# Moving setup evacuations, one filter copy and two output copies between VectorE, ScalarE and GpSimd in a fused FFT-filter and SwiGLU kernel

## The chip, the cores and the metric

The kernel runs on one core of a Trainium2 chip. The metric is the device time of one execution in microseconds (us); several executions are taken and their median is quoted. A trace comes from one profiled execution, and its "span" runs from the first to the last instruction, so that the time is some 1.7 to 2.4 us longer than the span.

In the profile the engines are called PE (TensorE matmuls), PEld (TensorE weight loads), DVE (VectorE), ACT (ScalarE), POOL (GpSimd) and SP (SyncE). A label such as L462 is a line of the kernel that was traced. The change adds three lines, so L569 of the kernel before is L572 of the changed one, and L578 is L581.

## The reference

Eight sequences of 3008 tokens with 256 features are filtered in the frequency domain. Each token then passes an RMS norm and a SwiGLU layer with 1536 hidden units.

```python
X = np.fft.rfft(x, axis=1)                      # x: 8 x 3008 x 256
y = np.fft.irfft(X * (filt_r + 1j * filt_i), n=3008, axis=1)
y = y.reshape(24064, 256)
xn = y / np.sqrt(np.mean(y * y, axis=-1, keepdims=True) + 1e-06) * rms_g
g = xn @ w_gate                                  # 256 x 1536
silu = g * (1.0 / (1.0 + np.exp(-g)))
out = (silu * (xn @ w_val)) @ w_out              # 1536 x 256
```

## The kernel before

The transforms are done in stages with small DFT matrices. For batch 0 they stand alone at the start ("the setup", up to some 60 us); those of the later batches are woven in between the SwiGLU matmuls of the batch ahead. The SwiGLU part takes the rest of the time and keeps TensorE full (in the trace below it is busy for 269.74 us of the 270 from 230 to 500 us).

In the setup, transposed groups `t1` are evacuated from PSUM to SBUF, stage B multiplies them on TensorE into `psb`, VectorE or GpSimd multiplies `psb` with the filter (`products`), and `bit_unit` (called by `inverses`) multiplies back on TensorE into `pgt`, which ScalarE evacuates into `gT`. The kernel keeps the filter on both halves of the partitions, so each chunk of it is duplicated by `f_dup`.

```python
def b_mm(b, i):                       # stage B of unit i
    ps = bank(3 if b else (0, 3, 4, 5)[i % 4], "psb").rearrange("p (a d) -> p a d", a=2)
    if b == 0 and i > 3:              # an idle matmul, overwritten by the real ones
        nc.tensor.matmul(ps[:, 0, :], wz[:, 0:P], wz[:, 0:D], start=True, stop=True)
    ...
def b_unit(b, i, ps=None):            # products of unit i
    ...
    eng = nc.vector
    if (i in (3, 5, 8, 12, 15)) if b else (i in (3, 7, 9, 12)):
        eng = nc.gpsimd
        ...
        nc.scalar.activation(out=v, in_=ps, func=AXT.Copy)   # GpSimd works on this copy
        ps = v
    eng.tensor_tensor(out=s1, in0=ps, in1=f1, op=ALU.mult)
    eng.tensor_tensor(out=s2, in0=ps, in1=f2, op=ALU.mult)
...
def f_dup(c, e, eng, lo=0, hi=KC):    # half of filter chunk c to the other partitions
    ...
    if eng is nc.scalar:
        eng.activation(out=t[a:a + HALF], in_=t[o:o + HALF], func=AXT.Copy)
    elif eng is nc.sync:
        eng.dma_start(t[a:a + HALF], t[o:o + HALF])
    else:
        eng.tensor_copy(out=t[a:a + HALF], in_=t[o:o + HALF])
...
def t1_copy(g, on_act):
    dst, ps = st[0]["t2"][g], st[0]["t2ps"].pop(g)
    if on_act:
        nc.scalar.activation(out=dst, in_=ps[0:KR], func=AXT.Copy)
    else:
        nc.vector.tensor_copy(out=dst, in_=ps[0:KR])
...
def down(b, m, jt, part):             # last matmul of a SwiGLU block
    ...
    if jt == JT - 1:
        o3 = late_p["op"].tile([P, 4, D], FP32, tag="o3", name="o3")
        if part is None:
            nc.scalar.activation(out=o3[:, 0:2, :], in_=po[0], func=AXT.Copy)
            nc.vector.tensor_copy(out=o3[:, 2:n, :], in_=po[1][:, 0:n - 2, :])
```

Of the kernel before, what the change touches and what calls it, by code (L numbers as in the profile page):

```python
# [12 lines left out]
AXT = mybir.ActivationFunctionType  # L13
# [108 lines left out]
def kernel(  # L122
# [11 lines left out]
    nc = tc.nc  # L134
# [109 lines left out]
    def b_unit(b, i, ps=None):  # L244
        if ps is None:
            ps = b_mm(b, i)
        f1, f2 = filt(2 * i, 2)
        if b:
            s1 = late_p["sp"].tile([P, 2, D], FP16, tag="s1", name="s1")
            s2 = late_p["sp"].tile([P, 2, D], FP16, tag="s2", name="s2")  # L250
            if summed(b, i):
                nc.vector.tensor_tensor(out=s1, in0=ps, in1=f1, op=ALU.mult)  # L252
                st[b]["s"][i] = (s1, s2, ps, f2)
                return
        elif i % 2:
            s1 = hp.tile([P, 512], FP16, tag="sg", name="sg").rearrange("p (a d) -> p a d", a=2)
            s2 = hhs[(i // 2) % 4].rearrange("p (a d) -> p a d", a=2)
        else:
            ss = xnp.tile([P, 2, 512], FP16, tag="xn", name="ss")
            s1, s2 = (ss[:, e, :].rearrange("p (a d) -> p a d", a=2) for e in range(2))  # L260
# [3 lines that stand above are left out]
            v = yp.tile([P, 2, 512], FP32, tag="y", name="v")  # L264
            v = v[:, 0, :].rearrange("p (a d) -> p a d", a=2)
            nc.scalar.activation(out=v, in_=ps, func=AXT.Copy)
# [3 lines that stand above are left out]
        st[b]["s"][i] = (s1, s2)  # L270
# [158 lines left out]
    def cut(b, m, part):  # L429
        return (0, nq(b, m)) if part is None else (2 * part, 2)  # L430
# [20 lines left out]
    def down(b, m, jt, part):  # L451
        hh = hh_of.pop((b, m, jt, part))
        if jt == 0:
            where = {None: ((psO, "po0"), (psO, "po1")), 0: ((psO, "po0"),), 1: ((psO, "po1"), (psM, "mx"))}
            po_of[(b, m, part)] = [pool.tile([P, 2, D], FP32, tag=tag, name=tag)
                                   for pool, tag in where[part]]
        po = po_of[(b, m, part)]

        n = cut(b, m, part)[1]
        per = 1 if part else 2  # L460
        for s4 in range(n):
            nc.tensor.matmul(po[s4 // per][:, s4 % per, :], hh[:, ts(s4, P)], wo[:, jt, :],  # L462
                             start=(jt == 0 and s4 % per == 0),
                             stop=(jt == JT - 1 and (s4 % per == per - 1 or s4 == n - 1)))
        if jt == JT - 1:
            o3 = late_p["op"].tile([P, 4, D], FP32, tag="o3", name="o3")
            if part is None:
                nc.scalar.activation(out=o3[:, 0:2, :], in_=po[0], func=AXT.Copy)
                nc.vector.tensor_copy(out=o3[:, 2:n, :], in_=po[1][:, 0:n - 2, :])  # L469
            else:  # L470
                nc.scalar.activation(out=o3[:, 0, :], in_=po[0][:, 0, :], func=AXT.Copy)
                nc.vector.tensor_copy(out=o3[:, 1, :], in_=po[part][:, 1 - part, :])
            po_of[(b, m, part)] = o3
# [38 lines left out]
    def f_dup(c, e, eng, lo=0, hi=KC):  # L512
        t = (fr, fi)[e][c][:, lo:hi, :]
        a, o = (0, HALF) if e else (HALF, 0)
# [6 lines that stand above are left out]
# [13 lines left out]
    def t1_mm(g):  # L534
        if g < 6:
            if g % 2 == 0:
                st[0]["t2t"] = t2p.tile([KR, KC, D], FP16, tag="t2", name="t2")
            dst = st[0]["t2t"][:, 4 * (g % 2):4 * (g % 2) + 4, :]
        else:
            dst = t3p.tile([KR, 4, D], FP16, tag="t3", name="t2")  # L540
        st[0]["t2"][g] = dst
        pool, tag = ((psG, "pg"), (psV, "pv"))[g % 2]
        ps = pool.tile([P, 4, D], FP16, tag=tag, name="pt1")
        af = aT.rearrange("p a k -> p (a k)")
        for a in range(4):
            for dh in range(2):
                b0 = dh * H * P
                src = af[:, b0:b0 + 32 * P].rearrange("p (i k) -> p k i", k=K2)[:, 4 * g + a, :]
                nc.tensor.transpose(ps[:, a, ts(dh, P)], src, ident)
        st[0]["t2ps"][g] = ps  # L550
# [8 lines that stand above are left out]
    def bit_unit(i):  # L559
        s1, s2 = st[0]["s"].pop(i)  # L560
        pair = i // 2
        closing = pair in st[0]["g"]
        if not closing:
            st[0]["g"][pair] = [bank((3 * dh) if pair == 7 else (1 + dh), "pgt") for dh in range(2)]
        for u in range(2):
            k = 2 * i + u
            for dh in range(2):
                o = st[0]["g"][pair][dh][:, ts(2 * (i % 2) + u, KR)]
                nc.tensor.matmul(o, s1[:, u, ds(dh * P, P)], wi_at(0, k)[:, 0:KR], start=True, stop=False)  # L569
                nc.tensor.matmul(o, s2[:, u, ds(dh * P, P)], wi_at(1, k)[:, 0:KR], start=False, stop=True)  # L570
        if closing:
            for dh in range(2):  # L572
                dst = gT[:, dh, pair * 4 * KR:(pair + 1) * 4 * KR]
                src = st[0]["g"][pair][dh][:, 0:4 * KR]
                if pair > 5 and dh:
                    nc.vector.tensor_copy(out=dst, in_=src)
                else:
                    nc.scalar.activation(out=dst, in_=src, func=AXT.Copy)  # L578
# [47 lines left out]
    def w_load(q):  # L626
        cols = ts(q, DFF // 3)
        for src, dst in ((moe_w_gate, wg), (moe_w_val, wv)):
            nc.gpsimd.dma_start(dst[:, :, cols], src.rearrange("(dt p) j -> p dt j", p=P)[:, :, cols])
        nc.gpsimd.dma_start(wo[:, ts(q, JT // 3), :],  # L630
                            moe_w_out.rearrange("(jt p) d -> p jt d", p=P)[:, ts(q, JT // 3), :])

    with tc.manual_schedule():
# [48 lines left out]
        A, G, S = nc.scalar, nc.gpsimd, nc.sync  # L682
        st[0]["t2ps"], st[0]["g"], psb = {}, {}, {}

        def products(*units):
            for i in units:
                b_unit(0, i, psb.pop(i))

        def stage_b(*units):
            for i in units:  # L690
                psb[i] = b_mm(0, i)

        def inverses(*units):
            for i in units:
                bit_unit(i)

        for g in range(4):
            t1_mm(g)
            t1_copy(g, g % 2)
        stage_b(0, 1, 2, 3)  # L700
        for g in range(4, 8):
            t1_mm(g)
        t1_copy(4, 0)
        f_dup(0, 0, A, 0, 2)
        f_dup(0, 1, G, 0, 2)
        f_dup(0, 0, A, 2, 4)
        f_dup(0, 1, G, 2, 8)
        f_dup(0, 0, A, 4, 8)
        products(0)
        stage_b(4)  # L710
        products(1)
# [23 lines left out]
        inverses(4)  # L735
        products(8)
        stage_b(12)
        inverses(5)
        f_dup(3, 1, A, 0, 4)
        products(12)  # L740
        w_load(0)
        w_load(1)
        products(10)
        stage_b(13, 14)
        inverses(6)
# [136 lines left out]
        for i in range(len(items) + 4):  # L882
            for fn, a in pre.get(i, ()):
                fn(*a)
            if i < len(items):
                gv(*items[i])
            for fn, a in plan.get(i, ()):
                fn(*a)
            if 2 <= i < len(items) + 2:
                down(*items[i - 2])  # L890
                if items[i - 2][2] == JT - 1:
                    stores[i + 1] = items[i - 2][:2] + items[i - 2][3:]
            for fn, a in late.get(i, ()):
                fn(*a)
            if i in stores:
                o_store(*stores[i])
# [30 lines left out]
```

## Time and profile before

| | kernel before |
|---|---|
| time, median of 3 executions | 889.63 us (889.43 to 890.09) |
| traced execution | 888.58 us, span 886.7 us |
| TensorE busy | 98% of the span |
| TensorE busy from 23.0 to 36.5 us | 8.83 of 13.5 us |
| TensorE waits for an output copy, whole span | 0.7 us, two times |

The page also divides the span into 40 slices. Of the kernel before I show the row of TensorE and the row of the granted clock, each digit a tenth of busy time or of full speed in one slice of some 22 us.

```profile
PE   8799999999999999999999999999999999999998
...
PEclk9999999999999999999999999999999999999999
```

Only the first two slices of TensorE and the last one are below 9: nearly all that can be won lies in the setup, with a few tenths in single places later.

### The profile page before, as it was taken

How to read it: one execution, taken by the hardware profiler on the slowest of the kernel's cores; microseconds unless marked ns; L12 is line 12 of the kernel's file. 1: busy time of each engine (PE TensorE's matmuls, PEld its weight loads, DVE VectorE, ACT ScalarE, POOL GpSimd, SP SyncE). 2: the span in 40 equal slices, each digit the busy share in tenths (PEclk: the TensorE clock that was granted, in tenths of full speed). 3: DMA queues.
4: the chain of work that ended last, by engine and by line, in shares of the span. 5: the costliest groups of instructions: out<-in, count | busy, mean ns of one | idle time of the engine just before them, and what ended most of it. 6: DMA issues, size and time to landing. Idle time of an engine off the chain costs nothing.

```text
span 886.7 us, 17463 instructions
## 1 busy us (share of the span) xinstructions
PE 873.2 (98%) x6257; PEld 559.0 (63%) x6257; DVE 678.7 (77%) x1088; ACT 625.3 (71%) x1069; POOL 436.5 (49%) x393
## 2 busy tenths in 40 slices
PE   8799999999999999999999999999999999999998
PEld 5566666666666666666666666666666666666556
DVE  7866786899888877888688887888878887555555
ACT  8878667677677766877677765887667765676444
POOL 7843941646527752667336661376515762155300
PEclk9999999999999999999999999999999999999999
DMA  9595736665653466343736346322352232222202
GB/s 201 118 197 156 163 78 209 143 141 122 177 141 82 101 141 173 93 100 101 193 86 143 85 90 183 93 91 84 99 152 75 64 90 71 77 66 49 72 24 48
DMA packets 80095, 101.44 MB, mean 114 GB/s; under 512 B 8108, under 2 KB 56684, under 8 KB 79560
## 3 DMA queue, kind: packets, MB, share of 16 engines
q1 hardware_dynamic: 69688, 84.23, 34.2%
q0 software_dynamic: 10240, 15.96, 11.5%
q8 instruction: 49, 0.80, 0.4%
q14 instruction: 38, 0.31, 0.1%
q10 hardware_dynamic: 80, 0.13, 0.1%
HBM read 67.67 MB, written 46.78 MB: 129 GB/s over the span
## 4 chain that ended last, share of the span: by engine, by line
PE 93%; DVE 1%; ACT 1%; issue 1%
PE po L462 27%; PE pg L443 27%; PE pv L443 27%; PE psi L291 3%; PE psb L238 3%; PE psn L323 2%; PE psa L203 2%; DVE o L469 1%; PE psq L352 1%; PE pt L589 0%; DVE hh L448 0%; ACT gT L578 0%; ACT fi L516 0%; PE psr L404 0%; PE pw L619 0%
## 5 line engine op out<-in xcount | busy, mean ns | idle before, releaser
L448 DVE TENSOR_TENSOR hh<-pv,sg 128x512 f16<-128x512 f32 (+2 forms) x588 | 392.8, 669 | 189.2 <-ACT sg L447 77.0
L447 ACT ACTIVATE sg<-pg 128x512 f16<-128x512 f32 (+2 forms) x588 | 340.8, 580 | 223.1 <-PE pg L443 213.6
L462 PE MATMUL po<-wo,hh 128*128 128x256 f16 x2244 | 342.6, 273 | 1.2 <-DVE o L469 0.7
L443 PE MATMUL pv<-xn,wv 128*128 128x512 f16 (+2 forms) x1176 | 339.9, 371 | 0.0
L443 PE MATMUL pg<-xn,wg 128*128 128x512 f16 (+2 forms) x1176 | 339.7, 370 | 0.0
L462 PEld LDWEIGHTS <-hh 128*128 128x128 f16 x2256 | 216.2, 97 | 96.8 <-issue 2.6
L282 POOL TENSOR_TENSOR s<-s,s 128x512 f16<-128x512 f16 x101 | 116.6, 1156 | 225.4 <-DVE s L276 156.6
L443 PEld LDWEIGHTS <-wv 128*128 128x128 f16 x1176 | 114.7, 98 | 128.9 <-issue 0.3
L419 POOL TENSOR_TENSOR xn<-y,rb 128x1024 f16<-128x1024 f32 (+1 forms) x45 | 126.1, 2802 | 52.5 <-DMA rb<-r_tmp 44.5
L443 PEld LDWEIGHTS <-wg 128*128 128x128 f16 x1176 | 111.2, 97 | 13.5 <-issue 0.3
L358 POOL TENSOR_TENSOR rho<-u,mhalf 128x4 f32<-128x4 f32 (+1 forms) x48 | 49.0, 1021 | 63.1 <-DVE u L356 62.9
L296 ACT ACTIVATE t<-psi 96x512 f16<-96x512 f32 x112 | 66.3, 592 | 8.3 <-PE psi L291 3.0
L276 DVE TENSOR_TENSOR s<-psb,fi 64x512 f16<-64x512 f32 x101 | 69.0, 683 | 3.0
L278 DVE SCALAR_TENSOR_TENSOR s<-psb,fi 64x512 f16<-64x512 f32 x101 | 69.9, 692 | 1.4
L329 ACT ACTIVATE y<-psn,gsb 128x512 f32<-128x512 f32 (+1 forms) x94 | 63.8, 678 | 7.8 <-PE psn L323 0.5
L252 DVE TENSOR_TENSOR s<-psb,fr 128x512 f16<-128x512 f32 x101 | 68.8, 681 | 0.0
L343 POOL TENSOR_TENSOR sq<-sq 128x512 f16<-128x512 f16 (+1 forms) x35 | 39.6, 1130 | 36.1 <-ACT sq L335 35.2
L335 ACT ACTIVATE sq<-psn 128x512 f16<-128x512 f32 (+1 forms) x94 | 54.8, 583 | 0.0
L208 ACT ACTIVATE t<-psa 128x512 f16<-128x512 f32 x70 | 41.8, 597 | 5.5 <-PE psa L203 2.4
L291 PE MATMUL psi<-s,wi 128*128 128x256 f16 x238 | 44.3, 273 | 0.0
L238 PE MATMUL psb<-t,wb 96*128 96x256 f16 x224 | 43.0, 273 | 0.3 <-DVE s L269 0.2
L323 PEld LDWEIGHTS <-t 128*128 128x128 f16 x368 | 28.3, 98 | 20.6 <-issue 0.4
(104 smaller groups left out, 526.2 us busy)
## 6 DMA issues: line engine op xcount, KB each, us to landing
out_dram<-o SPq DMA_DIRECT2D x83, 256.0 KB
xc<-in_x_dram POOLq DMA_DIRECT2D x56, 192.0 KB, 5.7
z_tmp<-t SPq DMA_DIRECT2D x28, 384.0 KB
t<-z_tmp SPq DMA_DIRECT2D x28, 384.0 KB
g_tmp<-t SPq DMA_DIRECT2D x56, 192.0 KB
rb<-r_tmp SPq DMA_DIRECT2D x41, 256.0 KB
t<-g_tmp SPq DMA_DIRECT2D x21, 384.0 KB
t<-g_tmp SPq DMA_DIRECT2D x7, 320.0 KB
```

Source lines behind the costliest of these rows:

```text
L238: nc.tensor.matmul(ps[:, u, :], w[:, k, :], t, start=True, stop=True)
L252: nc.vector.tensor_tensor(out=s1, in0=ps, in1=f1, op=ALU.mult)
L276: nc.vector.tensor_tensor(out=s2[a], in0=ps[e], in1=f2[e], op=ALU.mult)
L278: nc.vector.scalar_tensor_tensor(out=s2[a], in0=ps[e], scalar=-1.0, in1=f2[e], op0=ALU.mult, op1=ALU.mult)
L282: nc.gpsimd.tensor_tensor(out=s, in0=s1, in1=s2, op=ALU.add)
L291: nc.tensor.matmul(ps[:, u, :], wi_at(q, 2 * i + u), ss[q][:, u, :], start=(q == 0), stop=(q == n - 1))
L296: nc.scalar.activation(out=st[b]["t3"][c][:, 2 * r:2 * r + 2, :], in_=ps[0:KR], func=AXT.Copy)
L419: nc.gpsimd.tensor_tensor(out=xv, in0=yv, in1=rv.unsqueeze(1).to_broadcast([P, 2, n, P]), op=ALU.mult)
L443: nc.tensor.matmul(ps[:, 0:w], wt[:, dt_, ts(jt, P)], xn[:, dt_, :], start=(dt_ == 0), stop=(dt_ == 1))
L447: nc.scalar.activation(out=sg[:, 0:w], in_=pg[:, 0:w], func=AXT.Silu)
L448: nc.vector.tensor_tensor(out=hh[:, 0:w], in0=pv[:, 0:w], in1=sg[:, 0:w], op=ALU.mult)
L462: nc.tensor.matmul(po[s4 // per][:, s4 % per, :], hh[:, ts(s4, P)], wo[:, jt, :], start=(jt == 0 and s4 % per == 0), stop=(jt == JT - 1 an ...
```

## The change

The intent is to let the first filter product start sooner, to close an idle stretch of ScalarE near 32 us, and to take two output copies from VectorE at places where TensorE waits for them. Nothing is computed differently. The whole diff is short:

```diff
@@ down
                 nc.scalar.activation(out=o3[:, 0:2, :], in_=po[0], func=AXT.Copy)
-                nc.vector.tensor_copy(out=o3[:, 2:n, :], in_=po[1][:, 0:n - 2, :])
+                if (b, m) in ((0, 5), (1, 3)):
+                    nc.scalar.activation(out=o3[:, 2:n, :], in_=po[1][:, 0:n - 2, :], func=AXT.Copy)
+                else:
+                    nc.vector.tensor_copy(out=o3[:, 2:n, :], in_=po[1][:, 0:n - 2, :])
@@ the setup
         for g in range(4):
             t1_mm(g)
-            t1_copy(g, g % 2)
+            t1_copy(g, g == 1)
         stage_b(0, 1, 2, 3)
         for g in range(4, 8):
             t1_mm(g)
-        t1_copy(4, 0)
         f_dup(0, 0, A, 0, 2)
         f_dup(0, 1, G, 0, 2)
         f_dup(0, 0, A, 2, 4)
         f_dup(0, 1, G, 2, 8)
-        f_dup(0, 0, A, 4, 8)
+        t1_copy(4, 1)
+        f_dup(0, 0, G, 4, 8)
         products(0)
@@ further down in the setup
         stage_b(12)
-        inverses(5)
         f_dup(3, 1, A, 0, 4)
         products(12)
         w_load(0)
         w_load(1)
+        inverses(5)
         products(10)
```

Here A is ScalarE and G is GpSimd. I call the second hunk part 1, the third part 2 and the first part 3, as the prediction does.

## The prediction

The sum of the prediction is 0.77 us (parts 1 and 2) + 0.93 us (part 3) = 1.70 us, hence 887.9 us. Passages on the engines that no trace of this case shows are cut from it; none of them is a term of the sum. Where the text that is left gives 1.89 and 0.62 us beside ScalarE's 1.04, these are copies of the filter on GpSimd. That only the duplication of the filter could go to GpSimd was my assumption; no trace shows it.

> **What bounds the kernel now.** I first read the page's busy shares, then the busy time by stretches of the span, then TensorE's waits, then the two timelines around those waits.
>
> ```profile
> PE 873.2 (98%) x6257; PEld 559.0 (63%) x6257; DVE 678.7 (77%) x1088; ACT 625.3 (71%) x1069; POOL 436.5 (49%) x393
> PE 93%; DVE 1%; ACT 1%; issue 1%
> ```
>
> The chain that ended last is TensorE (PE) for 93% of the span. No other engine is full, so moving a copy from one engine to another can pay only where TensorE stands still. The stretches say where that is:
>
> ```profile
> core 0: us, PE busy (x) PEld busy (x) DVE busy (x) ACT busy (x) POOL busy (x), PEclk, DMA share, GB/s
> ...
> 17.60:23.00 5.40, 5.32 (x73) 5.04 (x72) 3.08 (x6) 3.79 (x5) 3.33 (x5) 1.00 0.80 208
> 23.00:36.50 13.50, 8.83 (x111) 6.62 (x110) 13.37 (x23) 12.38 (x20) 12.29 (x10) 1.00 0.52 123
> ...
> 160.00:230.00 70.00, 69.59 (x479) 43.73 (x478) 62.77 (x98) 51.70 (x89) 41.25 (x41) 1.00 0.62 145
> 230.00:500.00 270.00, 269.74 (x1860) 170.90 (x1858) 219.16 (x344) 199.03 (x339) 146.93 (x128) 1.00 0.49 122
> ```
>
> Between 23.0 and 36.5 us, the spectral setup of the first batch, TensorE is busy 8.83 of 13.5 us, VectorE (DVE) 13.37, ScalarE (ACT) 12.38 and GpSimd (POOL) 12.29: three engines almost full, TensorE waiting for them. After 60 us TensorE hardly waits at all. Its waits, all of them:
>
> ```profile
> PE psb L231 <- DVE ss L269: 2.2, 4, 0.8
> PE pgt L569 <- ACT gT L578: 1.3, 2, 1.1
> ...
> PE psb L231 <- DVE hh L269: 1.0, 2, 0.7
> PE po L462 <- DVE o L469: 0.7, 2, 0.4
> ```
>
> The fourth line is the only one of size in the steady part. The timeline puts its two cases at 162.81 and 237.64 us; counting blocks of output copies from 68.9 us, these are the ends of blocks (0,5) and (1,3), exactly the two that the change names.
>
> [...] the 128x512 fp32 output copy takes 597 ns on ScalarE and 681 ns on VectorE. It does not hold for every form: the 96x1024 fp16 copy t<-pt takes 1020 ns on ScalarE and 687 on VectorE, so these setup copies get dearer when moved to ScalarE. [...] the trace has 1.89 us for 64x2048 and 0.62 us for 64x512, while ScalarE needs 1.04 for 64x1024. [...]
>
> **Part 1, the early copies.** VectorE takes the fourth evacuation t1 (group 3, 0.69 us, its start-to-start slot 0.6) and gives away group 4 to ScalarE. The decisive thing is not the 0.6 us but the order: now VectorE stands 1.22 us waiting for group 4's transposes at 21.59 before the first filter product can start at 22.20.
>
> ```profile
> 19.69 0.69 DVE L557 COPY t<-pt 96x1024 f16<-96x1024 f16 x1 [0.33 <-PE pt L549]
> 21.59 0.69 DVE L557 COPY t<-pt 96x1024 f16<-96x1024 f16 x1 [1.22 <-PE pt L549]
> 22.20 0.68 DVE L268 TENSOR_TENSOR ss<-psb,fr 128x512 f16<-128x512 f32 x1
> ```
>
> In the changed order group 3 is copied at about 20.33 (the time ScalarE's second copy starts now) and the first product follows at about 20.95, if the first filter piece is there: ScalarE's duplication can start at 20.2 (end of its one t1 copy; by the landing events of the trace the first filter chunk is complete at 20.1) and ends 0.6 later. So VectorE gains about 1.25 us. ScalarE then does t1 copies 4 and 5 from 21.6 to 23.5 and the copy for the GpSimd product to about 24.05, against 24.89 now. The duplication moved to GpSimd falls in its idle 1.62 us before 22.76 (wait for the second chunk of fi): estimate 1.04 us from the two durations above, from 21.1 to 22.2, free.
>
> But I don't carry the 1.25 us on. The next ScalarE work is the duplication of the second chunk of fr, and by the landing events that chunk is complete only at 24.81; the SP queue's next load, which reuses its semaphore, also went out only at 24.83. Today the duplication starts at 24.97, so it can't come more than 0.1 us sooner. From there ScalarE is solid until 31.76 with the same list of work in both kernels (duplications, gT copies, v copies). VectorE will be earlier by about 0.9 us through this stretch (products(4) at about 26.05 instead of 26.98), but the thing that TensorE waits for at the end of the stage is ScalarE.
>
> **Part 2, inverses(5) moved down.** The order on TensorE is unchanged; on ScalarE the pair-2 gT copy moves behind the first duplication of fi chunk 3 and the v copy of unit 12.
>
> ```profile
> 31.16 0.60 ACT L266 ACTIVATE v<-psb 128x512 f32<-128x512 f32 x1
> 32.70 0.87 ACT L578 ACTIVATE gT<-pgt 128x384 f16<-128x384 f32 x2 [0.93 <-PE pgt L570]
> 33.59 1.06 ACT L516 ACTIVATE fi<-fi 64x1024 f32<-64x1024 f32 x1
> 34.55 0.57 ACT L266 ACTIVATE v<-psb 128x512 f32<-128x512 f32 x1
> 35.03 1.04 ACT L516 ACTIVATE fi<-fi 64x1024 f32<-64x1024 f32 x1
> 35.97 0.85 ACT L578 ACTIVATE gT<-pgt 128x384 f16<-128x384 f32 x2
> ```
>
> The 0.93 us of idleness goes: fi 31.78 to 32.8 (its chunk landed by 30.5), v to 33.35 (unit 12's products are ready because VectorE is now early), gT pair 2 to 34.2, fi to 35.2, gT pair 3 at 35.2 instead of 35.97. This last one releases TensorE's 1.14 us wait at 36.50. So TensorE goes on 0.77 us sooner. VectorE's last product, now ending at 38.04, ends near 37.15 and GpSimd's last near 36.85 instead of 37.70, so neither takes over. Behind this, up to the first gate matmul at 47.20, is one chain of TensorE and copies, and the weights, whose issue follows GpSimd's last product, move with it; the first gate weights had landed at 41.8. Parts 1 and 2 close the same idle stretch and are not to be added: with part 1 alone VectorE's product 8 ends near 30.9 instead of 31.84, inverses(5) follow by 31.8, and ScalarE need not wait either. Together: **-0.77 us**.
>
> **Part 3, the output copies.** At (0,5) TensorE issued two matmuls at 162.02, the third could go at 162.24 (spacing 0.11) and went at 162.81: 0.57 us lost, of which the wait list shows 0.41 because it counts from the modelled end. At (1,3): 237.22 became 237.64, 0.42 lost.
>
> ```profile
> 161.74 0.69 DVE L448 TENSOR_TENSOR hh<-pv,sg 128x512 f16<-128x512 f32 x1
> 162.34 0.41 DVE L469 COPY o<-po 128x256 f32<-128x256 f32 x1
> 162.81 0.38 PE L462 MATMUL po<-wo,hh 128*128 128x256 f16 x2 [0.41 <-DVE o L469]
> ```
>
> On ScalarE the second half follows the first at once: at 161.5 to 161.95 for (0,5), before 162.24, so all 0.57 is regained; at 236.65 to 237.23 for (1,3), so 0.06 remains and 0.36 is regained. The price is that the next sg starts 0.4 to 0.5 us later, and the hh after it about 0.25 later at (1,3) and no later at (0,5), where VectorE skips its copy. That hh is used two items, at least 1.8 us, further on. After (0,5) the next psb matmul (166.71) comes 0.62 us after the VectorE product it needs; with TensorE 0.57 earlier it just fits. **-0.93 us**.
>
> Sum: 0.77 + 0.93 = 1.70 us; 889.63 - 1.70 = 887.9 us. TensorE is full from there to the end, so an early start should be kept.
>
> **Rivals.** (a) VectorE, not ScalarE, holds the setup, since it is 99% busy there, and the whole 1.25 us comes through: then 0.5 us more, 887.4. For: the psb waits on VectorE are 3.2 us in all; against: the last wait of the stage is on gT. (b) The setup gain is hidden: a landing a few tenths later, the fi or v inputs late, or the t1 copies on ScalarE (1.02 us each) pushing the duplication back. Then only part 3 remains, 888.7. (c) Part 3 turns its wait into another: sg late, TensorE waits for hh or for the VectorE product after it. Then 0.3 to 0.6 us of part 3 return, 888.4. (d) Both fail: 889.6. For it: a tuned schedule with VectorE 90% busy between 160 and 230 us has little slack.
>
> **Range and chances.** The central case is 887.9; (a) to (c) span 887.4 to 888.7, and repeated runs differ by some 0.6 us (889.43 to 890.09). I take 886.9 to 889.2. Two per cent is 17.8 us; nothing here is a tenth of that, so within 2% has 0.98.
>
> **What would show it.** Right: no 1.22 us idle on VectorE near 21 us; the first product near 21.0; ScalarE's chunk-2 duplication still near 24.9; no 0.93 us idle near 32; gT pair 3 near 35.2; first gate matmul near 46.4; no wait of po L462 on an output copy above 0.1 us. Wrong: the first gate matmul still near 47.2 or as early as 45.9, a new TensorE wait on hh or sg near 163 or 239, or an early start that is gone again by 100 us.

## The result, and the profile after

| | before | changed |
|---|---|---|
| executions side by side, median | 889.53 us (889.28 to 890.09) | 886.72 us (885.73 to 887.87) |
| traced execution | 888.58 us, span 886.7 | 887.02 us, span 884.9 |

The ratio is 0.9968, with a 95% interval of 0.9951 to 0.9985; that is a real gain, far inside 2%. Ratios here and below are the mean time of one kernel's fast runs over that of the other's of the same rounds, so they are not quite the ratio of the medians that I quote. The class "within 2%" was right, but the median of 886.72 lies 0.18 us below the low end of my range.

First the page's busy line of the changed kernel, columns as before: TensorE works as long as it did, in a shorter span.

```profile
PE 873.1 (99%) x6257; PEld 559.7 (63%) x6257; DVE 678.2 (77%) x1086; ACT 625.1 (71%) x1070; POOL 437.9 (49%) x394
```

VectorE has two instructions less (its two output copies; the evacuation t1 of group 3 came and that of group 4 went), ScalarE one more and GpSimd one more. The busy time by stretches of the changed kernel, with the columns that the prediction's table has, shows where TensorE gained:

```profile
17.60:23.00 5.40, 5.34 (x74) 5.12 (x75) 3.84 (x7) 3.26 (x5) 3.81 (x6) 1.00 0.80 195
23.00:36.50 13.50, 9.27 (x125) 7.25 (x123) 12.98 (x23) 12.05 (x19) 13.22 (x10) 1.00 0.55 125
...
160.00:230.00 70.00, 70.00 (x483) 44.05 (x481) 62.99 (x98) 52.52 (x92) 41.38 (x41) 1.00 0.64 148
230.00:500.00 270.00, 270.00 (x1862) 171.41 (x1860) 219.14 (x344) 199.85 (x340) 148.13 (x128) 1.00 0.48 121
```

From 23.0 to 36.5 us it is busy 9.27 instead of 8.83 us and does 14 matmuls more. From 160 to 500 us it never stands. VectorE fell from 13.37 to 12.98 in the setup, and GpSimd rose from 12.29 to 13.22.

The list of TensorE's waits in the changed kernel (total, how often, longest):

```profile
PE pgt L572 <- ACT gT L581: 2.9, 2, 2.0
...
PE psb L231 <- DVE hh L269: 0.6, 1, 0.6
PE psb L231 <- DVE ss L269: 0.5, 1, 0.5
```

The wait for an output copy is gone. The waits of `psb` for VectorE fell from 3.2 us in all to 1.1 us, but the wait for ScalarE's `gT` rose from 1.3 to 2.9 us. The timeline of TensorE shows its two cases:

```profile
28.02 0.20 PE L572 MATMUL pgt<-wi,ss 128*128 128x96 f16 x1 [1.97 <-ACT gT L581]
...
35.55 0.20 PE L572 MATMUL pgt<-wi,ss 128*128 128x96 f16 x1 [0.90 <-ACT gT L581]
```

The first wait, at 28.02 us, is new. It costs nothing in the end, because the same chain must wait for ScalarE again later. The second is the one that I had named as the end of the stage: it was at 36.50 and is now at 35.55, **0.95 us sooner**. What releases it can be followed on ScalarE in the changed kernel:

```profile
20.73 1.17 ACT L519 ACTIVATE fr<-fr 64x512 f32<-64x512 f32 x2 [0.56 <-DMA fr<-in_filt_r_dram]
...
25.07 2.00 ACT L519 ACTIVATE fr<-fr 64x1024 f32<-64x1024 f32 x2 [0.72 <-DMA fr<-in_filt_r_dram]
...
31.89 1.06 ACT L519 ACTIVATE fi<-fi 64x1024 f32<-64x1024 f32 x1
32.85 0.58 ACT L266 ACTIVATE v<-psb 128x512 f32<-128x512 f32 x1
33.33 0.85 ACT L581 ACTIVATE gT<-pgt 128x384 f16<-128x384 f32 x2
34.07 1.05 ACT L519 ACTIVATE fi<-fi 64x1024 f32<-64x1024 f32 x1
35.02 0.85 ACT L581 ACTIVATE gT<-pgt 128x384 f16<-128x384 f32 x2
```

The idle 0.93 us near 32 us is gone. ScalarE waits twice for pieces of the filter, 0.56 us at 20.73 and 0.72 us at 25.07; the second is the landing that the prediction had named. And each of the last four instructions starts before the one ahead of it has ended by its recorded duration: the `fi` copy lasts 1.06 us, but the next starts 0.96 us after it; the `v` copy lasts 0.58, and the next starts 0.48 after it.

VectorE, in the changed kernel, starts the first product at 21.40 instead of 22.20:

```profile
19.66 1.28 DVE L560 COPY t<-pt 96x1024 f16<-96x1024 f16 x2 [0.35 <-PE pt L552]
21.40 0.69 DVE L268 TENSOR_TENSOR ss<-psb,fr 128x512 f16<-128x512 f32 x1 [0.45 <-ACT fr L519]
```

I had it at 20.95. The missing 0.45 us is the wait in brackets: it waits for ScalarE's duplication, and that waited 0.56 us for the first filter chunk, which I had taken to be there at 20.1.

At the end of block (0,5) ScalarE now does both halves of the output copy:

```profile
160.08 0.60 ACT L468 ACTIVATE o<-po 128x512 f32<-128x512 f32 x1
160.58 0.38 ACT L470 ACTIVATE o<-po 128x256 f32<-128x256 f32 x1
```

They follow at a distance of 0.50 us, and TensorE's next four `po` matmuls go at 161.08 without a stand. To see what each place is worth, I compared the start of the n-th TensorE matmul in the two traces (the order on TensorE is the same). The changed kernel is ahead by 0.95 us behind the wait at 35.55, by a further 0.57 us behind (0,5), a further 0.29 us behind (1,3), and by 1.81 us at the end. A small part of this, and of every such comparison, is the landing of x near 16 us, which differs by some tenths from execution to execution (here it is 0.03 us).

So the trace gained 1.81 us against a prediction of 1.70, and yet the median gained 2.8 to 2.9. The open question was therefore not the mechanism but the other microsecond.

### The profile page after: what moved, and what is told of

The parts are those of the page before. It is cut to its first block, busy times and chain, and to the rows that moved or that the text cites. A ratio compares the mean times of both kernels' runs of the same rounds, so it can differ in the third digit from the quotient of the medians.

```text
span 884.9 us, 17466 instructions
## 1 busy us (share of the span) xinstructions
PE 873.1 (99%) x6257; PEld 559.7 (63%) x6257; DVE 678.2 (77%) x1086; ACT 625.1 (71%) x1070; POOL 437.9 (49%) x394
## 4 chain that ended last, share of the span: by engine, by line
PE 94%; DMA 2%; DVE 1%; ACT 1%; POOL 1%; issue 1%; SPq 0%; ACTq 0%; POOLq 0%
PE po L462 27%; PE pg L443 27%; PE pv L443 27%; PE psi L291 3%; PE psb L238 3%; PE psn L323 2%; PE psa L203 2%; DMA fr<-in_filt_r_dram 2%; PE psq L352 1%; POOL xc L188 0%; DVE o L472 0%; ACT gT L581 0%; PE pt L592 0%; DVE hh L448 0%; ACT fi L519 0%
```

## The experiments

All kernels of one call ran on the same chip, beside runs of the kernel before; the calls were 1 (before_again, after_again, o_only, setup_only), 2 (p1_only, p2_only, before_less, after_less), 3 (p2_o, after_ref, after_fill, after_nofill), 4 (before_fill, p2_o_fill, before_t4, before_t5) and 5 (after_fill_b, after_c). All results were correct except for two kernels that were wrong. The medians of the kernel before were 889.5, 889.98, 889.96, 889.97 and 889.73 us in the five calls.

The summary comes first, since many runs are read together. "Full" counts the executions whose mean granted clock of TensorE, as a share of full speed, was at least 0.999, "low" those below; the last column is the median of the full ones alone.

| kernel | median us | ratio to before, 95% | full / low | median of full |
|---|---|---|---|---|
| before, all calls | 889.73 (67) | | 19 / 44 | 888.85 |
| changed, all calls | 887.45 (22) | see below | 13 / 9 | 887.02 |
| o_only | 888.36 | 0.9989, 0.9977 to 1.0001 | 3 / 2 | 888.01 |
| p1_only | 889.68 | 0.9990, 0.9974 to 1.0007 | 1 / 5 | 888.23 |
| p2_only | 887.86 | 0.9984, 0.9962 to 1.0007 | 5 / 1 | 887.85 |
| setup_only | 888.33 | 0.9982, 0.9970 to 0.9994 | 2 / 3 | 887.85 |
| p2_o | 888.80 | 1.0002, 0.9979 to 1.0024 | 0 / 6 | none |
| before_less | 889.49 | 1.0000, 0.9977 to 1.0023 | 3 / 3 | 888.88 |
| after_less | 886.98 | 0.9963, 0.9948 to 0.9979 | 4 / 2 | 886.98 |
| after_nofill | 888.48 | 0.9995, 0.9976 to 1.0015 | 0 / 6 | none |
| after_fill, two sets | 886.68 (10) | 0.9969 and 0.9972 | 8 / 2 | 886.53 |
| before_fill | 889.96 | 0.9989, 0.9962 to 1.0015 | 4 / 2 | 889.63 |
| p2_o_fill | 887.54 | 0.9964, 0.9936 to 0.9993 | 6 / 0 | 887.54 |

For four executions of the kernel before the clock is not on record. 0.999 counts as full because in most traces the clock also falls to half in the last 0.4 to 2.3 us of the span, after the last matmul (in the first trace of before it is 0.53 in the mean from 886.1 us to the end at 886.7); that alone takes up to 0.0013 off the mean and costs nothing. One warning on the split: it was made after the first results were seen, and a few groups are small.

### Do the two results come again? (before_again, after_again)

No edit: the two kernels as they are.

> The kernel before, unchanged, as a measure of noise and for a second trace. Theory 1 (the traces compared so far show the whole effect, 1.8 us; the other 1.0 us of the measured 2.8 us is scatter between executions): ratio 1.0000 within 0.0006, and the span of this trace lies between 886.7 and 887.7 us, with any difference from the first trace arising before 45 us, where loads land, not in the steady part. Theory 2 (the first trace of before was an unusually good execution; a usual one loses about 1 us more in the setup to a filter chunk that lands late): the trace of this run has the first gate matmul near 48.2 us, not 47.2.

> The changed kernel, unchanged. Theory 1: about 1.8 us under the kernel before (ratio 0.9980), since one trace against the other gives 0.95 us up to the first gate matmul, 0.57 at the end of block (0,5) and 0.29 at the end of block (1,3). Theory 2: 2.6 to 3.0 us again (0.9967 to 0.9971), because the reordered setup hides the late chunk too.

Measured: 889.75 us (ratio 1.0001, 0.9989 to 1.0013) and 887.43 us (0.9972, 0.9960 to 0.9985). The trace of before_again is 0.33 us behind the first one, all of it from the landing of x on, as theory 1 has it. The trace of after_again gains 0.74 (0.2 of it at the landing of x), 0.56 and 0.34 us at the three places and 1.65 us at the end. So the gain is there again, but at 2.1 to 2.3 us in the median it is smaller than the first 2.8; the ratio lies nearer to theory 2, the steps in the trace are those of theory 1. This trace also shows something that the first two do not: TensorE's clock stands at half for 6.8 us from 28.9 us on.

### Part 3 alone (o_only)

```diff
 in down(), on the kernel before:
+                if (b, m) in ((0, 5), (1, 3)):
+                    nc.scalar.activation(out=o3[:, 2:n, :], ...)
+                else:
                     nc.vector.tensor_copy(out=o3[:, 2:n, :], ...)
```

> Only the output copies of blocks (0,5) and (1,3) on ScalarE. Both theories: 0.86 us less (0.57 + 0.29, ratio 0.9990), nothing before 160 us. A rival that has these copies worth more, through VectorE work that gets free later on, needs over 1.3 us.

Measured: 888.36 us, ratio 0.9989 (0.9977 to 1.0001). In the trace nothing moves before 160 us except through the landing of x and the clock, and then it is 0.57 us at (0,5) and 0.34 us at (1,3), 0.91 in all, against 0.93 in the prediction. No wait of TensorE on `sg`, `hh` or a product takes their place around these blocks. But two waits come much later:

```profile
PE po L462 <- DVE hh L448: 0.5, 1, 0.5
PE po L462 <- DVE o L472: 0.3, 1, 0.3
```

The second is on an output copy near 822 us, the first lies at the very end. TensorE loses 0.22 us at each, so that of the 0.91 us about 0.5 are left at the end of this trace. p2_o and p2_o_fill below, which like this kernel have part 3 without part 1, show the same two waits and lose the same 0.45 us. No trace with both parts loses anything there; the changed kernel has only this:

```profile
PE po L462 <- DVE hh L448: 0.3, 1, 0.3
```

Why a change in the setup decides on waits at 820 us is not shown. By the three executions at full clock it is 888.01 against 888.85, which is 0.84 us. In this trace the clock stood at half for 3.4 us from 38.7 us, and TensorE fell back by 1.08 us there. This is why the traced execution, 889.45 us, is the slower sort: it hides the gain.

### Parts 1 and 2 without part 3 (setup_only)

```diff
 part 1 and part 2 of the change on the kernel before; down() as before
```

> Only the setup part of the change (copies, the piece on GpSimd, the later inverses(5)). Theory 1: 0.95 us less (ratio 0.9989). Theory 2: 1.7 to 2.1 us less (0.9976 to 0.9981). The first gate matmul near 46.25 us in its trace.

Measured: 888.33 us, ratio 0.9982 (0.9970 to 0.9994), clear of 1 by itself and, at 1.6 us, between the two theories. The traced execution gained only 0.21 us, of which 0.20 were there at the landing of x, and the timeline of ScalarE in this kernel says why:

```profile
32.63 1.06 ACT L516 ACTIVATE fi<-fi 64x1024 f32<-64x1024 f32 x1 [1.52 <-DMA fi<-in_filt_i_dram]
```

The third chunk of `fi` came late in this execution, and ScalarE stood for 1.52 us. With the distances that follow it (0.96, 0.48, 0.74 and 0.95 us from start to start, as in the changed kernel's trace) pair 3 comes at 35.76, just 0.21 us before the 35.97 of before. The change has made the setup tighter, so that it feels such a landing; the kernel before starts this copy at 33.59 in any case. Its executions at full clock, two only, have a median of 887.85.

### Part 1 alone and part 2 alone (p1_only, p2_only)

```diff
 p1_only: the second hunk of the change alone
-            t1_copy(g, g % 2)
+            t1_copy(g, g == 1)
 ...
-        t1_copy(4, 0)
-        f_dup(0, 0, A, 4, 8)
+        t1_copy(4, 1)
+        f_dup(0, 0, G, 4, 8)

 p2_only: the third hunk alone
-        inverses(5)
         f_dup(3, 1, A, 0, 4)
         products(12)
         w_load(0)
         w_load(1)
+        inverses(5)
```

> Only part 1: the early copies and the piece on GpSimd, without the later inverses(5). The prediction said that parts 1 and 2 close the same idle stretch of ScalarE, so each alone gives what both give: 0.8 us (ratio 0.9991). The landing theory (both together give more when a filter chunk lands early, because part 1 lets ScalarE start early and part 2 keeps it from waiting for inverses(5)) expects 0.5 to 0.9 us here, and less than for both together (about 1.6 us measured).

> Only part 2: inverses(5) behind the fi piece and products(12). Both theories: the 0.9 us idle of ScalarE near 32 us is gone, 0.6 to 0.9 us less (ratio 0.9990 to 0.9993), and no dependence on when the second filter chunk lands. Clock rival (the scatter and the extra come from TensorE running at half clock for some us of the setup): the time follows the granted clock of the run, not the parts.

Measured: p1_only 889.68 us (0.9990, 0.9974 to 1.0007), p2_only 887.86 us (0.9984, 0.9962 to 1.0007). Part 1 alone is not clear of zero, nor of the 0.8 us that I had credited to it. Two lines of ScalarE's timeline in p1_only:

```profile
22.44 1.15 ACT L516 ACTIVATE fr<-fr 64x512 f32<-64x512 f32 x2 [2.38 <-DMA fr<-in_filt_r_dram]
...
34.35 0.87 ACT L578 ACTIVATE gT<-pgt 128x384 f16<-128x384 f32 x2 [1.49 <-PE pgt L570]
```

The first filter chunk was late in this execution (the duplication starts at 22.44; 20.73 in the changed kernel), and the clock stood at half for 6.8 us from 26.8 us. The idle time ahead of `gT` pair 2 was 1.49 us, not closed. With such a disturbed trace I can't say whether part 1 alone closes it in a quiet execution.

Part 2 is clean. ScalarE in p2_only:

```profile
31.54 1.06 ACT L516 ACTIVATE fi<-fi 64x1024 f32<-64x1024 f32 x1
32.50 0.57 ACT L266 ACTIVATE v<-psb 128x512 f32<-128x512 f32 x1
...
34.67 0.85 ACT L578 ACTIVATE gT<-pgt 128x384 f16<-128x384 f32 x2
```

Pair 3 is at 34.67 instead of 35.97, which is 1.30 us; 0.20 of these were there already at the landing of x. TensorE gains 1.10 us behind that wait without any of part 1. At full clock the kernel stands at 887.85, which is 1.00 us under the kernel before. Part 2 therefore carries the gain of the setup. That of p2_only (1.00) and o_only (0.84) make 1.84; the whole change at full clock makes 888.85 - 887.02 = 1.83. By these groups, of five, three and thirteen executions, nothing is left for part 1 to add. The traces at full clock agree for the setup: behind the wait for pair 3, and without the landing of x, it is 1.10 us in p2_only, 0.92 in the first trace of the changed kernel and 1.2 in that of after_c. They disagree for the end: part 3 alone keeps about 0.5 us, with part 1 the whole of its 0.9.

### Is it the landing of the filter? (before_less, after_less)

Both kernels with fewer filter loads: of the chunks 1 to 3, where they go through SyncE's queue, the two loads of the odd rows are left out. The results are wrong (relative error 0.70 in before_less); the instructions on the compute engines are the same.

```diff
-        for g in range(2):
+        for g in range(0 if eng is nc.sync and c else 2):
             eng.dma_start(t[p0 + 1 + 24 * g: ...
```

> Wrong result on purpose: the kernel before, with the two mirrored pieces of filter chunks 1 to 3 on the SP queue left out, so these chunks land one or more us earlier. Landing theory: the kernel before does not use an early landing (ScalarE arrives at the chunk-2 copy at 24.9 us anyway), so within 0.4 us of before (ratio 0.9996 to 1.0004).

> Wrong result on purpose: the changed kernel with the same pieces left out. Landing theory: ScalarE starts the chunk copy near 24.1 instead of 24.9, the first gate matmul comes near 45.4 to 45.9, and the total is 2.2 to 3.0 us under before (ratio 0.9966 to 0.9975), with less scatter than the changed kernel. If instead the setup gain is 0.95 us whatever the landing, the total stays at 1.8 us under before (0.9980) and the gate matmul near 46.25.

Measured: 889.49 us (1.0000) and 886.98 us (0.9963, 0.9948 to 0.9979). At full clock they are 888.88 and 886.98, against 888.85 and 887.02 with all loads. Within its own call after_less is 3.0 us under the kernel before, and its first gate matmul comes at 45.71 us, both as the landing theory had said; but the changed kernel with all loads did not run in this call, so the comparison of the two goes across chips. In the trace of after_less `gT` pair 3 comes at 34.48 instead of 35.02; 0.35 us of this lead are lost again near 141 us, and the median at full clock is no lower. That a sooner landing of the filter is worth anything in the changed kernel is thus not shown. Late pieces cost something in single executions, as in setup_only, but no run here shows them to be the missing microsecond.

### Parts 2 and 3 without part 1 (p2_o), and the changed kernel beside it (after_ref)

```diff
 p2_o: first and third hunk; the second hunk left out.   after_ref: the changed kernel, no edit
```

> Part 2 and the output copies, without part 1. The traces so far give 1.10 us for part 2 alone (the whole wait for gT pair 3) and 0.86 for the output copies. If part 1 is worth nothing on top, this is 1.9 to 2.2 us under before (ratio 0.9975 to 0.9979) and within 0.5 us of the changed kernel in the same rounds, with fewer executions near 888. If part 1 carries the extra 0.8 us of the measured 2.6, this stays at 1.8 to 2.0 and the changed kernel beats it by 0.6 or more.

> The changed kernel again, for the same rounds and for a third trace. From its ten executions so far: two groups, 885.7 to 887.0 (six) and 887.9 to 888.0 (four). Clock theory: an execution of the slow group has a stretch of some us at granted clock 0.5 before 45 us, one of the fast group has none. Landing theory: the slow group has a filter chunk that lands late and clock 1.0.

Measured: p2_o 888.80 us (1.0002), after_ref 887.23 us (0.9972, 0.9960 to 0.9984). This looks as if part 1 were worth 1.6 us. But the trace of p2_o has all the steps: 0.73 us in the setup (0.21 of it at the landing of x), 0.57 at (0,5) and 0.34 at (1,3), for 887.41 us. Two things differ. One is the 0.45 us that p2_o, like o_only, loses again near 820 us and at the end. The other is the clock: all six executions of p2_o were low, with two at 891.75 and 894.69 us (clock 0.993 and 0.991), where four of six of after_ref were full.

What a half-clock stretch looks like is best seen where the kernel is the same and only the execution differs. In before_t4 (described below), an execution of the kernel before, the busy time in two slices of 3.4 us is the following, with the granted clock third from last:

```profile
27.50:30.90 3.40, 1.79 (x18) 1.28 (x19) 3.40 (x6) 3.35 (x7) 3.32 (x3) 1.00 0.87 176
30.90:34.30 3.40, 3.40 (x28) 2.80 (x26) 2.71 (x6) 1.52 (x5) 3.38 (x3) 0.50 0.19 41
```

The same slices of the first trace of the kernel before:

```profile
27.50:30.90 3.40, 1.58 (x17) 1.07 (x17) 3.40 (x7) 3.35 (x6) 3.26 (x4) 1.00 0.60 141
30.90:34.30 3.40, 3.13 (x47) 2.55 (x45) 3.27 (x6) 2.45 (x5) 3.40 (x3) 1.00 0.38 80
```

At a clock of 0.50 TensorE is busy all the time and gets through 28 matmuls instead of 47. The stretches seen in the setup have a clock of 0.50 and last 3.4 us (before_t4, o_only), 6.8 us (after_again, p1_only) or 13.7 us (after_nofill below). One of 3.4 us takes 3.4 x 0.5 / 887 = 0.0019 off the mean clock, so an execution with one reads 0.998, as before_t4 does, or 0.997 with the end of the span, as o_only does.

When the clock falls, the slices above do not say: ahead of the stretch TensorE was busier in before_t4 (1.79 us) than in the first trace (1.58 us), and only before_t4 fell to half. In the trace of after_nofill below, TensorE was busy for 0.83 and 1.36 us of the 3.4 us ahead of its two stretches; yet the first trace of the changed kernel has 3.4 us with only 1.42 us of busy time (from 24.65 us on) and no stretch. So quiet microseconds on TensorE alone are not enough for one. What else decides is not shown. That TensorE's activity has a say at all was my guess at this point; the next runs test it.

### Does TensorE's idle work in the setup decide the clock? (after_fill, after_nofill)

Stage B of batch 0 has one idle matmul ahead of the real ones from unit 4 on. after_fill does it three times; after_nofill leaves it out.

```diff
 after_fill, on the changed kernel:
         if b == 0 and i > 3:
-            nc.tensor.matmul(ps[:, 0, :], wz[:, 0:P], wz[:, 0:D], start=True, stop=True)
+            for _ in range(3):
+                nc.tensor.matmul(ps[:, 0, :], wz[:, 0:P], wz[:, 0:D], start=True, stop=True)
 after_nofill, on the changed kernel:
-        if b == 0 and i > 3:
-            nc.tensor.matmul(ps[:, 0, :], wz[:, 0:P], wz[:, 0:D], start=True, stop=True)
```

> The changed kernel with three idle matmuls in place of one ahead of each late stage-b pair (24 more, 0.11 us each, 2.6 us in all, most in TensorE's idle time). Clock theory: TensorE is busy enough, the stretches at half clock vanish and with them the group near 888; cost where the pair is waited for, up to 0.4 us. Landing theory: the two groups stay, everything 0.2 to 0.5 us later.

> The changed kernel without these idle matmuls (12 fewer). Clock theory: stretches at half clock in most executions, so most of them in the slow group or worse, median 888 or more. Landing theory: no slower than the changed kernel, perhaps 0.1 to 0.3 us faster, as each pair comes 0.11 us sooner.

Measured: after_fill 886.46 us (0.9969, 0.9957 to 0.9982) with one low execution of five, after_nofill 888.48 us (0.9995, 0.9976 to 1.0015) with six low of six. Two executions of after_nofill took 891.36 and 893.24 us. In its trace, the 893.24 us, the clock is at half for 13.7 us from 9.2 us on and for 3.4 us from 36.5 us on. The stretch at 36.5 us lies among the units that had idle matmuls (TensorE busy for 1.36 us of the 3.4 us before); the one at 9.2 us lies ahead of all of them, near the end of a load of `wbp` that takes 8.51 us of the critical chain, to 9.65 us (TensorE busy for 0.83 us of the 3.4 us before), so the edit can't be its cause. In this one trace, then, part of the loss is not of the edit's making. Six of six low against two of six of after_ref on the same chip has a probability of 0.03 by chance alone, which speaks for the idle matmuls holding the clock up. That p2_o, which has them, was all low in the same call says that they are not the whole of it.

### The same on the kernel before and on p2_o (before_fill, p2_o_fill), and two more looks at before (before_t4, before_t5)

```diff
 before_fill and p2_o_fill: the three idle matmuls of after_fill, on those kernels.
 before_t4, before_t5: the kernel before, no edit
```

> The kernel before with three idle matmuls in place of one ahead of each late stage-b pair. Clock theory: its usual executions lose about 1 us to half clock, so this gains 0.6 to 1.2 us (ratio 0.9987 to 0.9993). If the loss is elsewhere (landings, or outside of the traced span), it is 0 to 0.5 us slower than before.

> Part 2 and the output copies, with the same extra idle matmuls. Clock theory: the executions at 888.6 and above go, median 887.2 to 887.8. Else: unchanged near 888.8 or slower.

> The kernel before, for a further trace. Clock theory: where it is over 889.5 us, a stretch at granted clock 0.5 lies between 20 and 45 us. Landing theory: no such stretch, and the delay against the first trace appears at the transposes of x (16 us) or at a filter copy.

> As before_t4, one more trace of the kernel before: over 889.5 us either with a half-clock stretch (clock theory) or with a late x or filter transfer and none (landing theory).

Measured: p2_o_fill 887.54 us (0.9964, 0.9936 to 0.9993), none of six low, while nine of eleven executions of the kernel before in this call were; p2_o had had six of six low and no gain, in another call. before_fill 889.96 us (0.9989, 0.9962 to 1.0015), two of six low. The share of low executions fell on both, but the median of before_fill did not: at full clock it is at 889.63, 0.78 us above the kernel before, so by these four executions the extra matmuls cost by themselves in that kernel what the clock gave. The traced one shows less of it: its span is 0.2 us longer than that of the first trace. This is a miss, and it suggests that in this kernel the clock can't be mended for nothing.

p2_o_fill and after_fill differ by part 1 alone, and nearly all their executions are full: 887.54 against 886.53 us at full clock, so that with the extra matmuls part 1 is worth about 1.0 us (other chips, 6 and 8 executions). The traces of p2_o_fill and after_fill_b, which start alike, show 0.8 us of it in the setup and 0.4 us near 820 us and at the end. Without the extra matmuls no such gain is seen in the setup.

The two looks at the kernel before were both 889.26 us, so neither was over the 889.5 for which I had set an expectation, and yet they were not alike: before_t4 had the half-clock stretch shown above, before_t5 none. From the landing of x to behind the stretch before_t4 lost 0.88 us against the first trace. before_t5 took 0.68 us longer than the first trace, but its span is only 0.2 us longer: the rest lies outside of the span, which neither theory had foreseen. Four traces of the kernel before have a mean span of 887.03 us, four of the changed kernel 884.82 us; of the 2.21 us between them 0.2 are the landing of x.

### The changed kernel and after_fill again (after_c, after_fill_b)

No new edit: the changed kernel and after_fill on another chip.

> The changed kernel again, for these rounds: 886.9 to 887.4 us median, 2.2 to 3.0 us under before, as in its sixteen executions so far.

> The changed kernel with the extra idle matmuls again. If they are worth something: 0.4 to 0.9 us under the changed kernel of these rounds, no half-clock stretch between 20 and 45 us in the trace. If the first set was scatter: within 0.3 us of it.

Measured: after_c 888.16 us (0.9987, 0.9972 to 1.0002), with four of six low, which is a miss; after_fill_b 886.75 us (0.9972, 0.9960 to 0.9985), with one of five low, 1.4 us under the changed kernel where at most 0.9 was expected. The trace of after_c, at full clock, is one of the best of the changed kernel: 2.29 us ahead at the end. So on this chip the share of low executions was about that of the kernel before (8 of 11), and its median fell back to the edge of what can be told from before. The two sets of after_fill together, 886.68 us in 10 executions, are 0.78 us under the 22 of the changed kernel, with an interval from 1.43 less to 0.29 more: the lowest of all kernels, clear of the kernel before, but not proven better than the changed one.

## Why the prediction was wrong in the number and largely right in the mechanism

**What bounds the kernel.** This held. TensorE still ends the span, and every gain was read at a place where it stood.

**Part 1.** The argument that VectorE's earlier start is not carried on held for the whole change: the first product came 0.80 us sooner (1.25 predicted; the filter chunk landed later than assumed), ScalarE's chunk-2 duplication was at 25.07 (24.97 before, 24.9 predicted) and the stage was still ended by ScalarE. Rival (a) would have needed the 1.25 us at the end; it was 0.95 in the first trace, and p2_only gained its 1.10 us without VectorE's earlier start. That part 1 alone would close the idle stretch too is not shown: the only trace of it was disturbed by a late chunk and by the clock. At full clock, the medians of parts 2 and 3 measured apart already make up the whole gain. But the prediction credits part 1 with nothing beyond the setup, and there the traces contradict it: without part 1, part 3 loses 0.45 us again.

**Part 2** was mis-sized: predicted 0.77 us, measured 0.95 us in the first trace and 1.10 us in the trace of part 2 alone. The term that failed is the list "fi 31.78 to 32.8, v to 33.35, gT pair 2 to 34.2, fi to 35.2", in which I added recorded durations. What counted on the full ScalarE is the distance from start to start: 0.96 us for an `fi` copy of 1.06 us. With the distances of the trace (fi 0.96, v 0.48, the `gT` pair 0.74, fi 0.95) from 31.78, where I let the first `fi` copy start, pair 3 comes at 31.78 + 0.96 + 0.48 + 0.74 + 0.95 = 34.91, which is 1.06 us sooner than 35.97. The distances stood in the lines that the prediction shows: 33.59, 34.55, 35.03, 35.97. The first gate matmul came at 46.25 us, against 46.4 predicted. I had used such a distance for VectorE ("its start-to-start slot 0.6") and did not carry the thought over to ScalarE. In the traces the next instruction starts before the recorded end of the one ahead, by 0.10 us for an `fi` copy on ScalarE (1.06 us long, 0.96 apart) and by 0.08 us for a product on VectorE (0.68 us long, 0.60 apart).

**Part 3** held: predicted 0.57 and 0.36, measured 0.56 to 0.57 at (0,5) and 0.29 to 0.35 at (1,3) in the traces that have it, and in the changed kernel no wait took its place. At the very end of the span there is a wait of 0.3 us on `hh` that the list of before does not have, but the lead at the end, 1.81 us, is the sum of the three steps. Rival (c) came true where part 3 stood without part 1: 0.45 us came back, though at 820 us and at the end and not near the two blocks.

**The failed step** is the line "889.63 - 1.70 = 887.9 us". The 1.70 was worked out from one trace. That execution took 888.58 us at full clock, and I took the sum off a median of other executions, as if they were like it. They are not. Of 63 executions of the kernel before with a clock on record, 44 were low, with a median of 890.04 us (from 889.19), and 19 full, with a median of 888.85 us (to 890.17). All four executions of the changed kernel in the result were full. Had I taken my sum from the traced execution, it would have been 888.58 - 1.70 = 886.88 us, against 886.72 measured and 887.02 in the changed kernel's trace. Compared like with like, the change is worth 888.85 - 887.02 = 1.83 us at full clock and 890.04 - 888.00 = 2.04 us at low clock; the prediction's sum is short of these by 0.13 and 0.34 us, and the durations in part 2 alone are 0.29 us (35.20 against 34.91). The miss of 1.21 us is then 0.78 us from the starting point (889.63 against 888.85), 0.13 us from the sum, and 0.30 us of luck: the first four executions of the changed kernel were faster than its usual full ones (886.72 against 887.02).

I put the rest of the 2.8 us in the result down to the mixture of clocks and to this luck; for the four executions of before in it the clock is inferred from their times. Over all calls the medians differ by 2.28 us (bootstrap interval 1.70 to 2.99). My range was built from three executions of before, which "differ by some 0.6 us"; it had no place for a second sort of execution (and its "nothing here is a tenth of that" was wrong by its own rival (a), 2.2 us against 1.78), nor for the 0.9 to 1.1 us that a half-clock stretch cost in before_t4 and o_only, where nothing hid it. In after_ref, where one fell into a wait, the setup still gained 0.85 us, without the landing of x (0.92 and 1.2 in the two traces without a stretch).

**What stays open** is whether the change itself makes low executions rarer. Over all calls it had 9 of 22 low against 44 of 63, which by chance alone has a probability of about 0.02 in a one-sided exact test; but by sets it ran from none of four to four of six, and p2_only (one of six) and p2_o (six of six), whose setup is the same, lie as far apart as any two kernels. So the share also depends on the call. Taking the idle matmuls away (six of six low) and tripling them (two of ten) speak for TensorE's activity in the setup having a say in it; how much of the fall from 44 of 63 to 9 of 22 is due to the change can't be settled with these runs. The traces do not speak for it: the quietest 3.4 us between 7 and 50 us hold 1.4 to 1.6 us of busy TensorE in the four traces of the changed kernel and 1.6 in the four of before, but 2.1 in both of after_fill.

Open, too, is the time outside of the span. It was over 2.1 us in 31 of 63 executions of before, in three of six of p2_only and in three of six of before_fill, but in only one of 22 of the changed kernel and in none of p1_only, o_only, setup_only and p2_o (nor in before_less). In the mean this is 0.13 us in favour of the change, which no step of the prediction foresaw and no trace explains.

## What to carry to other kernels

Before subtracting a sum from a median, check that the traced execution is one of those that make the median: compare its time and its granted clock with theirs, and where there are two sorts, predict each by itself. On an engine that is full, add the distances from start to start, not the recorded durations; on ScalarE the durations of four instructions made pair 3 0.29 us late (35.20 against 34.91). When the expected gain is a quarter of a per cent, compare executions of the same clock, or the mixture will be taken for the effect, as nearly happened with p2_o. And follow the lead of a trace to its very end: parts of a change that look independent can meet hundreds of microseconds later, as here at 820 us.
